# Loading the first chunk of x transposed by DMA instead of transposing it on TensorE

## Chip, core and metric

The kernel runs on one core of one Trainium2 chip. The metric is the device time of one execution, in microseconds. The time of a kernel is the median of several executions.

## What is computed

A dense layer, SiLU, and a second dense layer, all in bf16:

```
x: [1, 2048, 640]    w1: [640, 1728]    w2: [1728, 640]

h   = einsum("bsd,df->bsf", x, w1)
h   = silu(h)                         # h * sigmoid(h)
out = einsum("bsf,fd->bsd", h, w2)    # [1, 2048, 640]
```

TensorE contracts over the 128 partitions of its two operands. For the first layer the contracted dimension is D = 640, five blocks of 128. So w1 can be loaded as it lies in memory, but x, whose rows are tokens, is needed transposed: D on the partitions, tokens along the free dimension. How the transposed x gets into SBUF for the first 512 tokens is what is changed.

## The kernel before

The names used below: P = 128, D = 640 (DT = 5 blocks), F = 1728 padded to FT = 14 blocks, S = 2048 tokens in NSC = 4 chunks of SCH = 512. `xT_sb` holds the transposed x, `w1_sb` and `w2_sb` the weights, `hT_sb` the activated hidden layer (hidden units on partitions), `ps1` four PSUM buffers of the first layer, `ps2` the PSUM of the second.

The first layer is a list of units. A unit computes one block of 128 hidden units for a stretch of tokens, with five accumulating matmuls. The first two blocks of chunk 0 are split in two halves of 256 tokens, so that work can begin on the first half:

```python
w1_groups = [(0, 2), (2, 4), (4, 8), (8, FT)]   # blocks of w1 loaded together
N_W1_ACT = 1                                    # groups loaded on the ScalarE queue
HN = SCH // 2
N_SPLIT_FT = 2
for ft in range(N_SPLIT_FT):
    units.append((0, ft, 0, HN))
TP_INSERT_AFTER = 0
for ft in range(N_SPLIT_FT):
    units.append((0, ft, HN, HN))
for ft in range(N_SPLIT_FT, FT):
    units.append((0, ft, 0, SCH))
# ... then all blocks of chunks 1, 2 and 3, 512 tokens each
```

TensorE first runs warm-up matmuls on zeros, which compute nothing that is used. Then it transposes the first chunk of x by multiplying with an identity matrix, two token blocks ahead of the first unit and two after it, and goes through the units:

```python
for i in range(N_WARM_MM):                      # 11, L246
    pe.matmul(ps1[:, NB1 - 1, :], lhsT=z_sb[:, 0:P], rhs=z_sb[:, :], start=True, stop=True)
...
def transpose_block(j):                         # L260
    if j % 2 == 0:
        pe.wait_ge(sem_x0[j // 2], 16)          # x half loaded
    for dt in range(DT):
        ins = pe.matmul(tp_views[wv][:, sl, :], lhsT=x0_sb[:, j, dt * P:(dt + 1) * P],
                        rhs=ident[:, :], start=True, stop=True)
    ins.then_inc(sem_tp, 1)
...
for i, (sc, ft, c0, n) in enumerate(units):
    # chunk 0: wait until VectorE and ScalarE have copied the transposed blocks
    # other chunks: wait for the five DMA transposes of the chunk
    # wait for the group of w1, and for a free PSUM buffer (sem_dve1)
    for dt in range(DT):                        # L295
        ins = pe.matmul(ps1[:, buf, 0:n], lhsT=w1_sb[:, dt, ft * P:(ft + 1) * P],
                        rhs=xT_sb[:, dt, col0:col0 + n], start=(dt == 0), stop=(dt == DT - 1))
    ins.then_inc(sem_pe1, 1)
    if i == TP_INSERT_AFTER:
        for j in range(hj, JB):
            transpose_block(j)
```

VectorE copies three of the five transposed blocks of each token block from PSUM to `xT_sb` (L414), ScalarE the other two (L363). For each unit ScalarE then computes the sigmoid (L372) and VectorE multiplies it with the matmul's result into `hT_sb` (L422), which also frees the PSUM buffer.

The loads are issued on two queues. SyncE's queue runs in order:

```python
sp.dma_start(out=x0_sb[:, 0:hj, :], in_=x0_v[:, 0:hj, :]).then_inc(sem_x0[0], 16)  # L182
sp.wait_ge(sem_x0[0], 16)
for gi in range(N_W1_ACT, len(w1_groups)):      # L189: groups 1, 2, 3
    load_w1_group(gi)
sp.wait_ge(sem_w1[W1_BIG], 16)                  # group 2 landed
for sc in range(1, NSC):
    x_chunk_transposes(sc)                      # L200: five DMA transposes of 512x128 each
    # after chunk 2: the three loads of w2
```

ScalarE's queue loads the second half of x's first chunk (L348) and group 0 of w1 (L353).

After all units the second layer runs (L335), 16 token tiles over 14 blocks, with its results copied out of PSUM by VectorE (L435, L447) and ScalarE (L384, L396) and stored.

Of the kernel before, what the change touches and what calls it, by code (L numbers as in the profile page):

```python
# [6 lines left out]
ALU = mybir.AluOpType  # L7


def bass_standalone__dense_activation_silu__prompt_kernel(  # L10
# [6 lines left out]
    bf16 = mybir.dt.bfloat16  # L17
    fp32 = mybir.dt.float32

    xf = x.flatten_outer_dims()  # L20
    of = out.flatten_outer_dims()
    S, D = xf.shape
    F = w1.shape[1]
    P = 128
    assert D % P == 0 and S % 512 == 0 and 512 < D <= 1024
    DT = D // P
    FT = (F + P - 1) // P
    FP = FT * P
    F_LAST = F - (FT - 1) * P
    ST = S // P  # L30
    SCH = 512
    NSC = S // SCH
    JB = SCH // P
    NB1 = 4
    NOB = 4
    DA = 512
    DB = D - DA
    assert ST >= 4 and ST % 2 == 0 and (ST - 2) % NOB + 1 == (ST - 1) % NOB
    assert JB % 2 == 0

    w1_groups = [(0, 2), (2, 4), (4, 8), (8, FT)]
    N_W1_ACT = 1
    W1_BIG = 2

    def w1_group_of(ft):
        for gi, (a, b) in enumerate(w1_groups):
# [2 lines left out]
        raise AssertionError  # L49

    HN = SCH // 2
    N_SPLIT_FT = 2
    units = []
    for ft in range(N_SPLIT_FT):
        units.append((0, ft, 0, HN))
    TP_INSERT_AFTER = 0
    for ft in range(N_SPLIT_FT):
        units.append((0, ft, HN, HN))
    for ft in range(N_SPLIT_FT, FT):
# [9 lines left out]
    n_w2_full = FT - 1 if F_LAST != P else FT  # L69
    w2_half = n_w2_full // 2  # L70
    n_w2_dmas = 3 if n_w2_full != FT else 2
    N_INIT = 4 if FP != F else 3
    N_WARM_MM = 11
    TPV = 3
    assert TPV <= 4 and DT - TPV <= 4

    TP_BANKS = {0: (1, 0), 1: (1, 8), 2: (0, 8), 3: (1, 0)}

    def tp_slot(j, dt):
        which, base = TP_BANKS[j % 4]  # L80
        slot = base + dt if dt < TPV else base + 4 + (dt - TPV)
        return which, slot

    with ExitStack() as es:
        def sb(name, shape, dtype):
            return es.enter_context(nc.sbuf_tensor(name, shape, dtype))
# [4 lines left out]
        def sem(name):  # L91
            return es.enter_context(nc.semaphore(name))

        xT_sb = sb("xT_sb", [P, DT, S], bf16)
# [2 lines left out]
        hT_sb = sb("hT_sb", [P, FT, S], bf16)  # L97
        sig_sb = sb("sig_sb", [P, NB1, SCH], bf16)
        o_sb = sb("o_sb", [P, NOB, D], bf16)
        x0_sb = sb("x0_sb", [P, JB, D], bf16)  # L100
        ident = sb("ident", [P, P], bf16)
        warm_sb = sb("warm_sb", [P, 32], fp32)
        z_sb = sb("z_sb", [P, SCH], bf16)
        ps1 = ps("ps1", [P, NB1, SCH], fp32)
        ps2 = ps("ps2", [P, 2, 1024], fp32)
        tp_views = [
            ps1[:, :, :].rearrange("p a (k s) -> p (a k) s", s=P),
            ps2[:, :, :].rearrange("p a (k s) -> p (a k) s", s=P),
        ]

        sem_init = sem("sem_init")
        sem_w2pad = sem("sem_w2pad")
        sem_z = sem("sem_z")
        sem_x0 = [sem(f"sem_x0_{i}") for i in range(JB // 2)]
        sem_x = [None] + [sem(f"sem_x{i}") for i in range(1, NSC)]
        sem_w1 = [sem(f"sem_w1_{i}") for i in range(len(w1_groups))]
        sem_w2 = sem("sem_w2")
        sem_o = [sem(f"sem_o{i}") for i in range(NOB)]
        sem_tp = sem("sem_tp")
        sem_tpc_v = sem("sem_tpc_v")  # L120
        sem_tpc_a = sem("sem_tpc_a")
        sem_pe1 = sem("sem_pe1")
        sem_act1 = sem("sem_act1")
        sem_dve1 = sem("sem_dve1")
# [4 lines left out]
        block = es.enter_context(nc.Block())  # L129

        w1_v = w1.rearrange("(dt p) f -> p dt f", p=P)
        x0_v = xf[0:SCH, :].rearrange("(j p) d -> p j d", p=P)
        w2_full_v = w2[0:n_w2_full * P, :].rearrange("(ft p) d -> p ft d", p=P)

        segs = []
# [21 lines left out]
        @block.gpsimd  # L157
        def _(pool):
            pool.memset(z_sb[:, SCH // 2:SCH], 0.0).then_inc(sem_z, 1)  # L159
            pool.memset(ident[:, :], 0.0).then_inc(sem_init, 1)  # L160
            pool.wait_ge(sem_init, 1)
            pool.affine_select(  # L162
                out=ident[:, :],
                in_=ident[:, :],
                compare_op=ALU.not_equal,
                fill=1.0,
                base=0,
                pattern=[[-1, P]],
                channel_multiplier=1,
            ).then_inc(sem_init, 1)  # L170
            if FP != F:
                pool.memset(w1_sb[:, :, F:FP], 0.0).then_inc(sem_init, 1)  # L172
            pool.memset(warm_sb[:, :], 0.0).then_inc(sem_init, 1)
            if FP != F:
                pool.memset(w2_sb[:, FT - 1, :], 0.0).then_inc(sem_w2pad, 1)  # L175
            else:
                pool.memset(warm_sb[:, 0:1], 0.0).then_inc(sem_w2pad, 1)

        @block.sync
        def _(sp):  # L180
            hj = JB // 2
            sp.dma_start(  # L182
                out=x0_sb[:, 0:hj, :], in_=x0_v[:, 0:hj, :]
            ).then_inc(sem_x0[0], 16)

            def load_w1_group(gi):
                a, b = w1_groups[gi]
# [2 lines left out]
                    out=w1_sb[:, :, f0:f1], in_=w1_v[:, :, f0:f1]  # L190
                ).then_inc(sem_w1[gi], 16)

            sp.wait_ge(sem_x0[0], 16)
            for gi in range(N_W1_ACT, len(w1_groups)):
                load_w1_group(gi)

# [5 lines left out]
                        in_=xf[s0:s0 + SCH, dt * P:(dt + 1) * P],  # L202
                    ).then_inc(sem_x[sc], 16)

            sp.wait_ge(sem_w1[W1_BIG], 16)
            for sc in range(1, NSC):
                x_chunk_transposes(sc)
                if sc == min(2, NSC - 1):
                    sp.dma_start(
                        out=w2_sb[:, 0:w2_half, :], in_=w2_full_v[:, 0:w2_half, :]  # L210
                    ).then_inc(sem_w2, 16)
                    sp.dma_start(
                        out=w2_sb[:, w2_half:n_w2_full, :],
                        in_=w2_full_v[:, w2_half:n_w2_full, :],
                    ).then_inc(sem_w2, 16)
                    sp.wait_ge(sem_w2pad, 1)
                    if n_w2_full != FT:
                        sp.dma_start(
                            out=w2_sb[0:F_LAST, FT - 1, :],
                            in_=w2[n_w2_full * P:F, :],  # L220
# [3 lines left out]
            for st in range(ST - 2):  # L224
# [4 lines left out]
                    out=of[st * P:(st + 1) * P, :], in_=o_sb[:, ob, :]  # L229
# [6 lines left out]
                in_=o_sb[:, obA:obA + 2, 0:DA],  # L236
# [6 lines left out]
        def _(pe):  # L243
# [8 lines left out]
                )  # L252
            pe.wait_ge(sem_init, N_INIT)

            def transpose_block(j):
                if j % 2 == 0:
                    pe.wait_ge(sem_x0[j // 2], 16)
                for dt in range(DT):
                    wv, sl = tp_slot(j, dt)
                    ins = pe.matmul(  # L260
                        tp_views[wv][:, sl, :],
                        lhsT=x0_sb[:, j, dt * P:(dt + 1) * P],
                        rhs=ident[:, :],
                        start=True,
                        stop=True,
                    )
                ins.then_inc(sem_tp, 1)

            hj = JB // 2
            for j in range(hj):  # L270
                transpose_block(j)

            w1_waited = set()
            x_waited = set()
            tpc_waited = 0
            for i, (sc, ft, c0, n) in enumerate(units):
                buf = i % NB1
                col0 = sc * SCH + c0
                if sc == 0:
                    jneed = (c0 + n - 1) // P + 1  # L280
                    if tpc_waited < jneed:
                        pe.wait_ge(sem_tpc_v, jneed)
                        pe.wait_ge(sem_tpc_a, jneed)
                        tpc_waited = jneed
                elif sc not in x_waited:
                    pe.wait_ge(sem_x[sc], 16 * DT)
                    x_waited.add(sc)
                gi = w1_group_of(ft)
                if gi not in w1_waited:
                    pe.wait_ge(sem_w1[gi], 16)  # L290
                    w1_waited.add(gi)
                if i >= NB1:
                    pe.wait_ge(sem_dve1, i - NB1 + 1)
                for dt in range(DT):
                    ins = pe.matmul(  # L295
                        ps1[:, buf, 0:n],
                        lhsT=w1_sb[:, dt, ft * P:(ft + 1) * P],
                        rhs=xT_sb[:, dt, col0:col0 + n],
                        start=(dt == 0),
                        stop=(dt == DT - 1),  # L300
                    )
                ins.then_inc(sem_pe1, 1)
                if i == TP_INSERT_AFTER:
                    for j in range(hj, JB):
                        transpose_block(j)

            pe.wait_ge(sem_w2pad, 1)
            pe.wait_ge(sem_w2, 16 * n_w2_dmas)
# [35 lines left out]

        @block.scalar
        def _(act):
            hj = JB // 2
            act.dma_start(  # L348
                out=x0_sb[:, hj:JB, :], in_=x0_v[:, hj:JB, :]
            ).then_inc(sem_x0[1], 16)  # L350
            for gi in range(N_W1_ACT):
                a, b = w1_groups[gi]
                act.dma_start(  # L353
# [3 lines left out]
            act.activation(  # L357
                out=warm_sb[:, :], in_=warm_sb[:, :], func=ACT.Sigmoid
            )
            for j in range(JB):  # L360
                wv, s0_ = tp_slot(j, TPV)
                act.wait_ge(sem_tp, j + 1)
                act.copy(  # L363
                    out=xT_sb[:, TPV:DT, j * P:(j + 1) * P],
                    in_=tp_views[wv][:, s0_:s0_ + (DT - TPV), :],
                ).then_inc(sem_tpc_a, 1)
            for i, (sc, ft, c0, n) in enumerate(units):
                buf = i % NB1
                act.wait_ge(sem_pe1, i + 1)
# [37 lines left out]
        @block.vector  # L407
        def _(dve):
            dve.memset(z_sb[:, 0:SCH // 2], 0.0).then_inc(sem_z, 1)  # L409
            dve.wait_ge(sem_init, N_INIT)  # L410
            for j in range(JB):
                wv, s0_ = tp_slot(j, 0)
                dve.wait_ge(sem_tp, j + 1)  # L413
                dve.tensor_copy(  # L414
                    out=xT_sb[:, 0:TPV, j * P:(j + 1) * P],
                    in_=tp_views[wv][:, s0_:s0_ + TPV, :],
                ).then_inc(sem_tpc_v, 1)
            for i, (sc, ft, c0, n) in enumerate(units):
                buf = i % NB1
                col0 = sc * SCH + c0  # L420
# [58 lines left out]
```

## Time and profile before

| | before |
|---|---|
| device time, median of 4 | 134.41 us (133.53 to 134.57) |
| span of the profiled execution | 132.8 us |
| PE busy | 127.2 us (96%) |
| first layer's matmuls, L295 | 60.7 us |
| second layer's matmuls, L335 | 60.6 us |
| VectorE busy | 52.0 us (39%) |
| ScalarE busy | 40.5 us (31%) |

PE is TensorE's matmul, PEld its loading of the stationary operand, DVE is VectorE, ACT ScalarE, POOL GpSimd, SP SyncE. A name with q, such as SPq, is the engine's queue of instructions, here the issuing of DMA transfers. Times in the profile count from the start of the span. The profile has a chain of work: from the last instruction of the run it goes back, step by step, to whatever each one waited for. What lies on it sets the time; what lies beside it doesn't, however long it is. Where the profile says "issue" the engine waited for nothing it shows. The times "to landing" count from the issue of a transfer to its completion.

### The profile page before, as it was taken

How to read it: one execution, taken by the hardware profiler on the slowest of the kernel's cores; microseconds unless marked ns; L12 is line 12 of the kernel's file. 1: busy time of each engine (PE TensorE's matmuls, PEld its weight loads, DVE VectorE, ACT ScalarE, POOL GpSimd, SP SyncE). 2: the span in 40 equal slices, each digit the busy share in tenths (PEclk: the TensorE clock that was granted, in tenths of full speed). 3: DMA queues.
4: the chain of work that ended last, by engine and by line, in shares of the span. 5: the costliest groups of instructions: out<-in, count | busy, mean ns of one | idle time of the engine just before them, and what ended most of it. 6: DMA issues, size and time to landing. Idle time of an engine off the chain costs nothing.

```text
span 132.8 us, 1876 instructions
## 1 busy us (share of the span) xinstructions
PE 127.2 (96%) x755; PEld 65.8 (50%) x769; DVE 52.0 (39%) x78; ACT 40.5 (31%) x79; POOL 1.9 (1%) x10
## 2 busy tenths in 40 slices
PE   6969999999999999999999999999999999999992
PEld 2445444444444444444445555555555555555461
DVE  0065666666666666666662222222012222220121
ACT  4054555555555555555550000000000000000001
POOL 5000000000000000000000000000000000000000
PEclk9999999999999999999999999999999999999999
DMA  3898454699400000000000111011111110111103
GB/s 112 250 363 217 110 67 105 168 376 278 82 2 0 5 0 2 0 0 0 0 0 5 49 49 49 15 40 49 49 49 49 54 49 7 42 49 54 49 0 99
DMA packets 15672, 9.78 MB, mean 74 GB/s; under 512 B 8816, under 2 KB 15664, under 8 KB 15664
## 3 DMA queue, kind: packets, MB, share of 16 engines
q1 hardware_dynamic: 14464, 8.95, 23.9%
q10 hardware_dynamic: 1200, 0.72, 1.8%
q8 instruction: 6, 0.10, 0.3%
q14 instruction: 2, 0.02, 0.0%
HBM read 5.08 MB, written 2.62 MB: 58 GB/s over the span
## 4 chain that ended last, share of the span: by engine, by line
PE 95%; DVE 2%; issue 1%; ACT 0%; POOL 0%; DVEq 0%; POOLq 0%
PE ps L335 46%; PE ps L295 45%; PE ps L246 4%; DVE xT_sb L414 2%; PE ps L260 1%; ACT o_sb L396 0%; POOL z_sb L159 0%; DVEq L413 0%; POOLq L464 0%
## 5 line engine op out<-in xcount | busy, mean ns | idle before, releaser
L295 PE MATMUL ps<-xT_sb,w_sb 128*128 128x512 bf16 (+1 forms) x284 | 60.7, 372 | 1.5 <-DVE xT_sb L414 1.2
L335 PE MATMUL ps<-w_sb,hT_sb 128*128 128x512 bf16 (+1 forms) x440 | 60.6, 298 | 0.4
L335 PEld LDWEIGHTS ps<-w_sb,hT_sb 128*128 128x128 bf16 x448 | 34.5, 98 | 26.7
L422 DVE TENSOR_TENSOR hT_sb<-ps,sig_sb 128x512 bf16<-128x512 f32 (+1 forms) x58 | 39.0, 674 | 22.0 <-ACT sig_sb L372 21.9
L295 PEld LDWEIGHTS ps<-xT_sb,w_sb 128*128 128x128 bf16 x290 | 28.2, 98 | 33.5 <-DVE xT_sb L414 1.7
L372 ACT ACTIVATE sig_sb<-ps 128x512 bf16<-128x512 f32 (+1 forms) x58 | 33.7, 583 | 27.0 <-PE ps L295 27.0
L435 DVE CAST o_sb<-ps 128x512 bf16<-128x512 f32 x14 | 9.7, 692 | 42.9 <-PE ps L335 42.9
L384 ACT CAST o_sb<-ps 128x128 bf16<-128x128 f32 x14 | 3.7, 266 | 49.2 <-PE ps L335 49.2
L246 PE MATMUL ps<-z_sb 128*128 128x512 bf16 x11 | 4.9, 632 | 1.1 <-POOL z_sb L159 1.1
L414 DVE CAST xT_sb<-ps 128x384 bf16<-128x384 f32 x4 | 2.0, 553 | 6.7 <-PE ps L260 6.7
L447 DVE CAST o_sb<-ps 128x1024 bf16<-128x1024 f32 x1 | 1.2, 1225 | 5.3 <-PE ps L335 5.3
L246 PEld LDWEIGHTS ps<-z_sb 128*128 128x128 bf16 x11 | 1.5, 143 | 3.6 <-issue 2.5
L363 ACT CAST xT_sb<-ps 128x256 bf16<-128x256 f32 x4 | 1.3, 373 | 4.8 <-PE ps L260 4.8
L396 ACT CAST o_sb<-ps 128x256 bf16<-128x256 f32 x1 | 0.4, 373 | 7.3 <-PE ps L335 7.3
L260 PEld LDWEIGHTS ps<-ident,x_sb 128*128 128x128 bf16 x20 | 1.6, 116 | 0.6 <-issue 0.6
L357 ACT ACT_TABLE_LOAD x1 | 1.3, 1283 | 1.8 <-issue 1.8
L260 PE MATMUL ps<-ident,x_sb 128*128 128x128 bf16 x20 | 1.7, 245 | 0.0
L175 POOL MEMSET w_sb<- 128x640 bf16 x1 | 0.6, 632 | 0.0
L409 DVE MEMSET z_sb<- 128x128 uint32 x1 | 0.2, 165 | 0.8 <-PEq L464 0.8
L172 POOL MEMSET w_sb<- 128x320 bf16 x1 | 0.4, 365 | 0.0
L159 POOL MEMSET z_sb<- 128x256 bf16 x1 | 0.3, 312 | 0.3 <-POOLq L464 0.3
L162 POOL TENSOR_SCALAR_AFFINE_SELECT ident<-ident 128x128 bf16<-128x128 bf16 x1 | 0.3, 295 | 0.2 <-POOL ident L160 0.2
(7 smaller groups left out, 1.0 us busy)
## 6 DMA issues: line engine op xcount, KB each, us to landing
out_dram<-o_sb SPq DMA_DIRECT2D x14, 160.0 KB, 1.8
w_sb<-in_w_dram SPq DMA_DIRECT2D x1, 1120.0 KB, 8.3
w_sb<-in_w_dram SPq DMA_DIRECT2D x1, 960.0 KB, 5.5
w_sb<-in_w_dram SPq DMA_DIRECT2D x1, 880.0 KB, 6.7
w_sb<-in_w_dram SPq DMA_DIRECT2D x1, 640.0 KB, 4.6
x_sb<-in_x_dram SPq DMA_DIRECT2D x1, 320.0 KB, 3.7
x_sb<-in_x_dram ACTq DMA_DIRECT2D x1, 320.0 KB, 4.1
w_sb<-in_w_dram ACTq DMA_DIRECT2D x1, 320.0 KB, 4.5
```

The costliest lines, as they stand in the source:

```text
L246: pe.matmul(ps1[:, NB1 - 1, :], lhsT=z_sb[:, 0:P], rhs=z_sb[:, :], start=True, stop=True,)
L260: ins = pe.matmul(tp_views[wv][:, sl, :], lhsT=x0_sb[:, j, dt * P:(dt + 1) * P], rhs=ident[:, :], start=True, stop=True,)
L295: ins = pe.matmul(ps1[:, buf, 0:n], lhsT=w1_sb[:, dt, ft * P:(ft + 1) * P], rhs=xT_sb[:, dt, col0:col0 + n], start=(dt == 0), stop=(dt == ...
L335: ins = pe.matmul(ps2[:, b2, c0:c0 + ncol], lhsT=hT_sb[:, ft, st * P:(st + 1) * P], rhs=w2_sb[:, ft, d0:d0 + ncol], start=(ft == 0), stop= ...
L357: act.activation(out=warm_sb[:, :], in_=warm_sb[:, :], func=ACT.Sigmoid)
L363: act.copy(out=xT_sb[:, TPV:DT, j * P:(j + 1) * P], in_=tp_views[wv][:, s0_:s0_ + (DT - TPV), :],).then_inc(sem_tpc_a, 1)
L372: act.activation(out=sig_sb[:, buf, 0:n], in_=ps1[:, buf, 0:n], func=ACT.Sigmoid,).then_inc(sem_act1, 1)
L384: act.copy(out=o_sb[:, ob, DA:D], in_=ps2[:, b2, c0:c0 + ncol]).then_inc(sem_ev_a, 1)
L414: dve.tensor_copy(out=xT_sb[:, 0:TPV, j * P:(j + 1) * P], in_=tp_views[wv][:, s0_:s0_ + TPV, :],).then_inc(sem_tpc_v, 1)
L422: dve.tensor_tensor(out=hT_sb[:, ft, col0:col0 + n], in0=ps1[:, buf, 0:n], in1=sig_sb[:, buf, 0:n], op=ALU.mult,).then_inc(sem_dve1, 1)
L435: dve.tensor_copy(out=o_sb[:, ob, 0:DA], in_=ps2[:, b2, c0:c0 + ncol]).then_inc(sem_ev_v, 1)
L447: dve.tensor_copy(out=o_sb[:, obA:obA + 2, 0:DA], in_=ps2[:, bA_, 0:2 * DA].rearrange("p (t c) -> p t c", t=2),).then_inc(sem_ev_v, 1)
```

## The change

The first 512 tokens of x are loaded already transposed, in two DMA transposes of 256 tokens by 640, as the other chunks are loaded transposed in five transfers of 512 by 128. The purpose is to take the transposing off TensorE, and the copies out of PSUM off VectorE and ScalarE, at the start of the kernel. The identity matrix, its making on GpSimd, the staging tensor `x0_sb` and their semaphores go away. Four things are adjusted with it: four blocks instead of two are split into halves of 256 tokens, four more warm-up matmuls run, group 1 of w1 moves from SyncE's queue to ScalarE's, and SyncE no longer waits for transfers to land before it issues the next ones.

```diff
-    N_W1_ACT = 1
-    W1_BIG = 2
+    N_W1_ACT = 2
...
-    N_SPLIT_FT = 2
+    N_SPLIT_FT = 4
...
-    N_INIT = 4 if FP != F else 3
-    N_WARM_MM = 11
+    N_INIT = 2 if FP != F else 1
+    N_WARM_MM = 15
...
         @block.sync
-            hj = JB // 2
-            sp.dma_start(
-                out=x0_sb[:, 0:hj, :], in_=x0_v[:, 0:hj, :]
-            ).then_inc(sem_x0[0], 16)
+            for h in range(2):
+                r0 = h * HN
+                sp.dma_start_transpose(
+                    out=xT_sb[:, :, r0:r0 + HN],
+                    in_=xf[r0:r0 + HN, :].rearrange("s (dt p) -> s dt p", p=P),
+                ).then_inc(sem_xc0[h], 16)
...
-            sp.wait_ge(sem_x0[0], 16)
             for gi in range(N_W1_ACT, len(w1_groups)):
                 load_w1_group(gi)
...
-            sp.wait_ge(sem_w1[W1_BIG], 16)
             for sc in range(1, NSC):
                 x_chunk_transposes(sc)
...
         @block.tensor
-            def transpose_block(j):
-                ... (the identity matmuls)
-            hj = JB // 2
-            for j in range(hj):
-                transpose_block(j)
...
                 if sc == 0:
-                    jneed = (c0 + n - 1) // P + 1
-                    if tpc_waited < jneed:
-                        pe.wait_ge(sem_tpc_v, jneed)
-                        pe.wait_ge(sem_tpc_a, jneed)
-                        tpc_waited = jneed
+                    for h in range(c0 // HN, (c0 + n - 1) // HN + 1):
+                        if ("c0", h) not in x_waited:
+                            pe.wait_ge(sem_xc0[h], 16)
+                            x_waited.add(("c0", h))
...
-                if i == TP_INSERT_AFTER:
-                    for j in range(hj, JB):
-                        transpose_block(j)
...
         @block.scalar
-            act.dma_start(
-                out=x0_sb[:, hj:JB, :], in_=x0_v[:, hj:JB, :]
-            ).then_inc(sem_x0[1], 16)
...
-            for j in range(JB):
-                ... act.copy of two transposed blocks to xT_sb
...
         @block.vector
-            dve.wait_ge(sem_init, N_INIT)
-            for j in range(JB):
-                ... dve.tensor_copy of three transposed blocks to xT_sb
```

In the changed kernel the warm-up matmuls are L211, the first layer's L240, and the transposed loads of chunk 0 L148.

More of the change, by code (lines that the diff above doesn't have):

```diff
@@ L32, in bass_standalone__dense_activation_silu__prompt_kernel @@
     NSC = S // SCH
-    JB = SCH // P
     NB1 = 4
@@ L38, in bass_standalone__dense_activation_silu__prompt_kernel @@
     assert ST >= 4 and ST % 2 == 0 and (ST - 2) % NOB + 1 == (ST - 1) % NOB
-    assert JB % 2 == 0
     w1_groups = [(0, 2), (2, 4), (4, 8), (8, FT)]
-    N_W1_ACT = 1
-    W1_BIG = 2
+    N_W1_ACT = 2
     def w1_group_of(ft):
@@ L55, in bass_standalone__dense_activation_silu__prompt_kernel @@
         units.append((0, ft, 0, HN))
-    TP_INSERT_AFTER = 0
     for ft in range(N_SPLIT_FT):
@@ L71, in bass_standalone__dense_activation_silu__prompt_kernel @@
     n_w2_dmas = 3 if n_w2_full != FT else 2
-    N_INIT = 4 if FP != F else 3
-    N_WARM_MM = 11
[L74 to L82, printed above, removed]
+    N_INIT = 2 if FP != F else 1
+    N_WARM_MM = 15
     with ExitStack() as es:
@@ L99, in bass_standalone__dense_activation_silu__prompt_kernel @@
         o_sb = sb("o_sb", [P, NOB, D], bf16)
-        x0_sb = sb("x0_sb", [P, JB, D], bf16)
-        ident = sb("ident", [P, P], bf16)
         warm_sb = sb("warm_sb", [P, 32], fp32)
@@ L105, in bass_standalone__dense_activation_silu__prompt_kernel @@
         ps2 = ps("ps2", [P, 2, 1024], fp32)
[L106 to L109, printed above, removed]
         sem_init = sem("sem_init")
@@ L113, in bass_standalone__dense_activation_silu__prompt_kernel @@
         sem_z = sem("sem_z")
-        sem_x0 = [sem(f"sem_x0_{i}") for i in range(JB // 2)]
+        sem_xc0 = [sem(f"sem_xc0_{i}") for i in range(2)]
         sem_x = [None] + [sem(f"sem_x{i}") for i in range(1, NSC)]
@@ L118, in bass_standalone__dense_activation_silu__prompt_kernel @@
         sem_o = [sem(f"sem_o{i}") for i in range(NOB)]
-        sem_tp = sem("sem_tp")
-        sem_tpc_v = sem("sem_tpc_v")
-        sem_tpc_a = sem("sem_tpc_a")
         sem_pe1 = sem("sem_pe1")
@@ L131, in bass_standalone__dense_activation_silu__prompt_kernel @@
         w1_v = w1.rearrange("(dt p) f -> p dt f", p=P)
-        x0_v = xf[0:SCH, :].rearrange("(j p) d -> p j d", p=P)
         w2_full_v = w2[0:n_w2_full * P, :].rearrange("(ft p) d -> p ft d", p=P)
@@ L159, in _ @@
             pool.memset(z_sb[:, SCH // 2:SCH], 0.0).then_inc(sem_z, 1)
[L160 to L170, printed above, removed]
             if FP != F:
@@ L253, in _ @@
             pe.wait_ge(sem_init, N_INIT)
-            def transpose_block(j):
[L256 to L267, printed above, removed]
-            hj = JB // 2
-            for j in range(hj):
-                transpose_block(j)
             w1_waited = set()
             x_waited = set()
-            tpc_waited = 0
             for i, (sc, ft, c0, n) in enumerate(units):
@@ L346, in _ @@
         def _(act):
-            hj = JB // 2
-            act.dma_start(
-                out=x0_sb[:, hj:JB, :], in_=x0_v[:, hj:JB, :]
-            ).then_inc(sem_x0[1], 16)
             for gi in range(N_W1_ACT):
@@ L359, in _ @@
             )
-            for j in range(JB):
[L361 to L366, printed above, removed]
             for i, (sc, ft, c0, n) in enumerate(units):
@@ L409, in _ @@
             dve.memset(z_sb[:, 0:SCH // 2], 0.0).then_inc(sem_z, 1)
-            dve.wait_ge(sem_init, N_INIT)
-            for j in range(JB):
[L412 to L417, printed above, removed]
             for i, (sc, ft, c0, n) in enumerate(units):
```

## The prediction

> **What bounds the kernel now.** I read the chain that ended last first, because it says what the end of the run hangs on.
>
> ```profile
> PE 95%; DVE 2%; issue 1%; ACT 0%; POOL 0%; DVEq 0%; POOLq 0%
> PE ps L335 46%; PE ps L295 45%; PE ps L246 4%; DVE xT_sb L414 2%; PE ps L260 1%; ACT o_sb L396 0%; POOL z_sb L159 0%; DVEq L413 0%; POOLq L464 0%
> ```
>
> The reader is to see that 91% of the span is the two layers' matmuls (L295 and L335), which the change leaves alone. Only the small terms can move: warm-up matmuls (L246), identity transposes (L260) and copies out of PSUM (L414), about 7% together. All of these lie in the first 10 us, so I took the same chain in order of time there (start, length, what).
>
> ```profile
> 1.10 4.87 PE ps L246 x11
> 5.97 0.55 PE ps L260 x5
> ...
> 6.62 1.03 DVE xT_sb L414 x2
> 7.65 0.04 issue
> 7.70 0.72 PE ps L295 x5
> 8.42 0.29 PE ps L260 x5
> ...
> 8.73 1.03 DVE xT_sb L414 x2
> 9.77 0.05 issue
> 9.81 1.26 PE ps L295 x10
> ```
>
> The warm-up ends, TensorE transposes, VectorE copies for a microsecond, TensorE does one unit (five matmuls), transposes again, VectorE copies for another microsecond. Only from 9.81 us does layer 1 run without a gap. Ten 256-column matmuls are done by then. A 512-column matmul takes 0.216 us in the steady part: the chain's pieces of L295 repeat every 10.79 us, for 50 matmuls each (49 have a record). Half of it, 0.108 us, times ten is 1.08 us. So the start is worth as much as an unbroken layer 1 from 9.81 - 1.08 = **8.73 us**. I call this the effective start; a microsecond off it is a microsecond off the time, as nothing later waits: layer 1's only idle time ahead of TensorE is 1.2 us, all on these copies.
>
> Next the SyncE queue in the timeline (start, time the queue was held) and the transfers' landing times in the page, for the new first transfers.
>
> ```profile
> 0.73 0.46 SPq L182 DMA_DIRECT2D x_sb<-in_x_dram  x1
> 4.46 1.52 SPq L189 DMA_DIRECT2D w_sb<-in_w_dram  x3
> 9.52 13.86 SPq L200 DMA_TRANSPOSE xT_sb<-in_x_dram  x10
> ```
>
> ```profile
> w_sb<-in_w_dram SPq DMA_DIRECT2D x1, 640.0 KB, 4.6
> xT_sb<-in_x_dram SPq DMA_TRANSPOSE x15, 3.1
> ```
>
> A DMA transpose of 512x128 holds the queue for 1.26 us in the median, where a plain transfer holds it about 0.5 us. It lands about 2.7 us after its start where little else moves (those issued from 12 to 15 us and from 19 to 23 us), and 3.1 in the median of all.
>
> The last view is a table of windows (columns: window and its length, PE, PEld, DVE, ACT and POOL busy, clock, DMA share, GB/s), for how fast the DMA engines can transpose.
>
> ```profile
> 22.00:23.00 1.00, 1.00 (x5) 0.41 (x5) 0.61 (x2) 0.52 (x2) 0.00 (x0) 1.00 0.57 130
> 27.00:28.00 1.00, 1.00 (x7) 0.42 (x5) 0.61 (x2) 0.60 (x1) 0.00 (x0) 1.00 1.07 376
> 33.00:34.00 1.00, 1.00 (x6) 0.42 (x5) 0.67 (x1) 0.52 (x2) 0.00 (x0) 1.00 1.10 215
> ```
>
> Paced by the queue, transposes move 130 GB/s with the engines 57% busy. With a backlog (33 us) they reach 215 GB/s; plain loads (27 us) reach 376.
>
> [...] warm-up weight loads are 0.43 us apart (the loads at 4.06, 4.49 and 4.91 us), twice 0.216. The first ten identity transposes show the switch: nine of their weight loads fill 0.84 us, so eight intervals of 0.0925 us, between the cold 0.107 (a quarter of 0.428) and the 0.061 of the second ten (0.65 us for ten). Solving 0.107 n + 0.061 (8 - n) = 0.74 gives n = 5.5, so full clock from about 5.77 + 5.5 x 0.107 = 6.36 us.
>
> [...] transposes beside the w2 loads took 6.6 and 7.8 us.
>
> [...]
>
> **The change part by part.**
>
> *Removed from the path.* Twenty identity matmuls and eight copies go, with both waits of TensorE on VectorE.
>
> *Warm-up, 11 to 15 matmuls.* At 0.4275 us each the eleven end at 1.10 + 4.70 = 5.80 us. If the clock switches at 6.36, 1.3 of the four added ones run cold and 2.7 take 0.216 us: the array comes free at 6.36 + 0.59 = **6.95 us**. All cold it would be 7.51 us; with an early switch at about 4.5, 8 cold and 7 warm end at 6.0.
>
> *First half of x.* It is 256x640, 2.5 times the elements of a 512x128 transfer. Its issue is either proportional, 2.5 x 1.26 = 3.15 us, or a fixed 0.5 (the plain transfers) plus 2.5 x 0.76 = 2.4 us. Landing came 2.7 - 1.26 = 1.45 us after the issue ended. So 0.73 + (2.4 to 3.15) + 1.45 = 4.6 to 5.3 us undisturbed. Groups 0 and 1 of w1 (0.65 MB at 376 GB/s, 1.75 us of all engines) run beside it; if half of that delays it, about 5.5 to 6.2 us. That is ahead of 6.95, so the wait ends with the warm-up.
>
> *Second half.* Its issue ends at 0.73 + (4.8 to 6.3), it lands at 7.0 to 8.5 us, up to 9 with contention. TensorE has four units on the first half, 20 x 0.108 = 2.16 us, and asks for it at 6.95 + 2.16 = 9.11 us. This is what N_SPLIT_FT = 4 buys: it covers the second transfer. The margin is thin.
>
> *w1 group 2* is issued after both transposes, at 5.5 to 7.0 us. In the kernel before it landed 1.9 us after group 1, which took 3.2 alone for 0.33 MB (0.87 us at 376): 2.3 fixed plus 1.75 is 4.05 us, so 9.6 to 11.1 us. It is needed after eight half units, at 6.95 + 40 x 0.108 = 11.27 us. Again thin. Group 3 has 2.35 us more of data, at most 13.5 us, and is needed at 15.6.
>
> *Later chunks.* Chunk 1's five transposes follow at about 8 us and land by about 16; they are needed one quarter of layer 1 (15.1 us) after the start, at 22. ScalarE (0.386 us per half unit) and VectorE (0.422) stay under TensorE's 0.54 us. Ten whole matmuls become twenty halves, for 0.04 us.
>
> *Sum.* The effective start goes from 8.73 to 6.95, a gain of 1.78 us. I take off 0.1 for the thin margins and get 134.41 - 1.7 = **132.7 us**, 1.3% less.
>
> **The rivals.**
>
> 1. *The transposed load becomes the start's bound.* The wait for VectorE is replaced by one for the DMA. If the 3D transpose costs 4 us of issue, or the first transfers after launch are slower, the halves land at about 6.9 and 10.9; the effective start is then 10.9 - 2.16 = 8.7 and the gain is nothing: 134.4 us. For it: no transpose of this shape is in the trace, and DMA was at full share from 3 to 5 us before. Against it: needed are 9.1 us, and the same bytes at 215 GB/s are 3.05 us plus 1.75 for w1, 4.8 us of transfer from 1.9 us on.
> 2. *w1 group 2 comes late.* Sharing the queue behind two long transposes, it may land at 12 us: a stall of 0.7 us, 133.4 us. For it: it waits for the queue and for bandwidth. Against it: before, it landed at 9.6 having been issued at 5.0.
> 3. *The transposed load is far slower than its share* (5 us or more each, or slowed again by the neighbouring loads as beside w2, 7.8 us): halves at 8 and 13 us, effective start about 11, 136.7 us. Only this reaches a loss near 2%, and nothing but the w2 contention speaks for it.
> 4. *The warm-up costs less.* With the clock switched early, TensorE is free at 6.0, about when the load arrives: a gain of 2.7, or 131.8 us with the same 0.1 off. The same early switch would speed the kernel before too, whose times spread from 133.53 to 134.57.
>
> **Range and chances.** The path has a floor: no load makes TensorE free before about 6.0 to 7.5 us, so the gain is bounded by about 2.7 us, and 2% (2.69 us, below 131.7) is at its very edge. The other side is open, to about no gain where the load decides. So 131.7 to 134.2, faster by over 2% with chance 0.09, within 2% 0.86, slower 0.05.
>
> **What would show it.** In the chain after, the warm-up is 15 matmuls and L240 (the layer-1 matmul there) follows it by 7.0 us, without VectorE between. The transposes hold the queue 2.4 to 3.15 us each. If the first L240 starts well after the last warm-up, or there is a gap after 20 or 40 half matmuls, rival 1 or 2 holds. Layer 2's first matmul, 69.35 us before, should stand near 67.6. A different length of either layer from there would make the whole reckoning wrong.

## The result, and the profile after

| | before | after |
|---|---|---|
| device time, median | 134.26 us (16 runs, 133.28 to 134.60) | 132.94 us (11 runs, 132.79 to 133.18) |
| ratio after to before | | 0.991 (0.9888 to 0.9932) |
| span of the profiled execution | 132.8 us | 131.4 us |
| first matmul of layer 2 | 69.35 us | 67.93 us |

The change gained 1.3 us, 0.9%. The prediction was 132.7 us. The times after lie within 0.4 us of each other, those before within 1.3 us; this turned out to be the clue to what holds the start now.

The chain of the kernel after, shares by engine and by line:

```profile
PE 97%; issue 1%; ACT 0%; POOL 0%; POOLq 0%
PE ps L277 46%; PE ps L240 46%; PE ps L211 5%; ACT o_sb L327 0%; POOL z_sb L135 0%; POOLq L387 0%
```

VectorE is off the chain, and the warm-up's share went from 4 to 5%. The same chain in order of time (start, length, what):

```profile
1.10 6.34 PE ps L211 x15
7.45 4.37 PE ps L240 x40
11.81 0.05 issue
11.86 10.74 PE ps L240 x49
...
67.93 5.43 PE ps L277 x40
```

The chain counts an overlap of two matmuls to the first of them, and their ends are modelled. Layer 1's first matmul began a little earlier, as TensorE's timeline shows (start, length, engine, what):

```profile
7.28 4.96 PE L240 MATMUL ps<-xT_sb,w_sb 128*128 128x256 bf16 x41
```

Layer 1 follows the warm-up and has no gap after 20 or 40 half matmuls. Both layers have their old length: layer 1 takes 60.65 us from 7.28 to the start of layer 2, and took 60.62 from the effective start of 8.73; layer 2's matmuls are 60.6 us as before. So the whole gain lies ahead of layer 1, as expected. The transfers of the kernel after, from the queue's timeline and from the view of the transposed loads' line (queue held, minimum/median/maximum in ns; then landing):

```profile
0.73 4.11 SPq L148 DMA_TRANSPOSE xT_sb<-in_x_dram  x2
4.89 1.44 SPq L156 DMA_DIRECT2D w_sb<-in_w_dram  x2
```

```profile
L148 SPq DMA_TRANSPOSE xT_sb<-in_x_dram x2: 1357/2026/2695, 0.7 to 2.1; - x2
...
DMA to landing us min/median/max: 5.7/6.0/6.3
```

The first half was issued at 0.73 and landed 6.3 us later, at **7.04 us**; the second, issued at 2.15, landed at 7.84. The first is much later than the 5.5 to 6.2 us of the prediction, and close to the 7.28 us at which layer 1's first matmul began. From this view alone one can't tell whether the load or the warm-up let TensorE go. The trace's records of single packets show where the load was. A half of x is 1280 pieces of 256 bytes, a group of w1 640 pieces of 512 bytes:

```
us            x, SyncE's queue (packets)    w1, ScalarE's queue (packets)
1.5 to 3.5              0                        467   group 0
3.5 to 4.5            681   first half           173   group 0
4.5 to 5.5            597   first half           315   group 1
5.5 to 6.0              5                        304   group 1
6.0 to 7.5           1277   second half           21   group 1
completion of the first half: 6.88 to 7.04; of group 1: 6.71 to 6.82
```

No packet of x moved before 3.5 us, when three quarters of group 0 of w1, issued at the same time on the other queue, had passed. The first half's data were through at 5.5 us, but its completion came 1.3 to 1.5 us later, just after that of group 1.

### The profile page after: what moved, and what is told of

It is laid out like the page before. It is cut to its first block, busy times and chain, and to the rows that moved or that the text cites. A ratio compares the mean times of both kernels' runs of the same rounds, so it can differ in the third digit from the quotient of the medians.

```text
span 131.4 us, 1854 instructions
## 1 busy us (share of the span) xinstructions
PE 126.9 (97%) x749; PEld 65.9 (50%) x763; DVE 50.5 (38%) x76; ACT 39.8 (30%) x77; POOL 1.5 (1%) x8
## 4 chain that ended last, share of the span: by engine, by line
PE 97%; issue 1%; ACT 0%; POOL 0%; POOLq 0%
PE ps L277 46%; PE ps L240 46%; PE ps L211 5%; ACT o_sb L327 0%; POOL z_sb L135 0%; POOLq L387 0%
## 5 line engine op out<-in xcount | busy, mean ns | idle before, releaser
L277 PE MATMUL ps<-w_sb,hT_sb 128*128 128x128 bf16 (+1 forms) x440 | 60.6, 298 | 0.4
L240 PE MATMUL ps<-xT_sb,w_sb 128*128 128x512 bf16 (+1 forms) x294 | 60.3, 365 | 0.3
L240 PEld LDWEIGHTS ps<-xT_sb,w_sb 128*128 128x128 bf16 x300 | 29.4, 98 | 31.3 <-issue 0.3
L211 PE MATMUL ps<-z_sb 128*128 128x512 bf16 x15 | 6.3, 615 | 1.1 <-POOL z_sb L135 1.1
L211 PEld LDWEIGHTS ps<-z_sb 128*128 128x128 bf16 x15 | 2.1, 146 | 4.7 <-issue 3.6
```

Of the source, the lines that this page charges most:

```text
L277: ins = pe.matmul(ps2[:, b2, c0:c0 + ncol], lhsT=hT_sb[:, ft, st * P:(st + 1) * P], rhs=w2_sb[:, ft, d0:d0 + ncol], start=(ft == 0), stop= ...
```

## The experiments

Two theories stood against each other. **A**, the prediction's: the warm-up sets the start, the load is in time. **B**: the transposed load, at 7.0 us, sets it wherever the warm-up ends earlier. A third, **C**, gave the gain to the earlier issue of the loads. Ratios are to the kernel before on the same chip, with their 95% intervals.

**Fewer warm-up matmuls.**

```diff
-    N_WARM_MM = 15
+    N_WARM_MM = 11
```

> The changed kernel with 11 warm-up matmuls instead of 15. Theory A (the warm-up sets the start, the load is in time): TensorE starts layer 1 at about 5.9 us, cold, and the time falls to about 132.3. Theory B (the first transposed half, which landed at 7.04 us in the trace of the changed kernel, sets the start as much as the warm-up): TensorE stands still from 5.8 to about 7.1 us, nothing is gained, 132.9 us[...].

Measured: 132.98 us, 0.9913 (0.9882 to 0.9945), as with 15. The chain:

```profile
1.10 4.05 PE ps L211 x11
5.15 1.86 issue
7.01 4.53 PE ps L240 x40
```

The warm-up ended at 5.15 us, the first half of x landed at 6.92, and layer 1 began at 7.01. TensorE stood still for 1.86 us, which the chain calls "issue" because it found nothing to put it down to; the landing just before it says what it was. B holds: where the warm-up ends early, the load sets the start, here 0.09 us after it landed. In the trace of the changed kernel itself the same 0.09 us after the landing would be 7.13 us, but layer 1 began at 7.28: the clock, by the trace's record of it, switched only at 7.07, and the warm-up still ended last, by about 0.15 us.

One of the eight runs took 134.38 us, and two versions below have one such run each (134.34 us among 15 runs, 134.86 us among 22). Those runs have no trace, and the cause is not shown.

**Plain loads in place of the transposed ones.** The 512 tokens are left untransposed.

```diff
-                sp.dma_start_transpose(
+                sp.dma_start(
                     out=xT_sb[:, :, r0:r0 + HN],
-                    in_=xf[r0:r0 + HN, :].rearrange("s (dt p) -> s dt p", p=P),
+                    in_=xf[r0:r0 + HN, :].rearrange("(p a) d -> p (a d)", p=P).rearrange(
+                        "p (dt s) -> p dt s", s=HN),
```

> The changed kernel with the two transposed loads of chunk 0 replaced by plain loads of the same bytes into the same place; the transposition of these 512 tokens is left out, so the output differs from the reference. Theory A (the warm-up alone sets the start): same time as the changed kernel, 132.9 us. Theory B (the transposed load holds the start wherever the warm-up ends earlier): the load lands at about 5 us, the start is set by the warm-up, whose end varies with the moment of the clock's switch, and the times spread again as those of the kernel before do, over about a microsecond below 133.1; median about 132.5.

Measured: 132.65 us (131.57 to 133.13), 0.987 (0.9833 to 0.9906). The chain of its profiled execution, which took 131.57 us:

```profile
1.10 4.71 PE ps L212 x15
5.81 4.42 PE ps L241 x40
```

The first half landed at 5.59 us, and layer 1's first matmul began at 5.68, just as the last one of the warm-up made way (the chain has 5.81). The spread of 1.6 us is back. So the narrow band of the changed kernel is the mark of the load: it arrives at about 7.0 us whenever the clock switches (7.04 with the switch at 7.07, and 7.00 with one at 4.57 in a trace below), and hides the early switches that this run can use. The plain load, too, moved no packet before 3.5 us, so that part of the delay is not the transposing.

**Two split blocks.**

```diff
-    N_SPLIT_FT = 4
+    N_SPLIT_FT = 2
```

> The changed kernel with two blocks split into halves instead of four, so that the second half of x is asked for one microsecond earlier, at about 8.4 us. The prediction's step (four split blocks cover the second transfer, whose margin is thin) with the landing it estimated, 8.5 to 9: a wait of 0.1 to 0.6 us, 133.1 to 133.5 us. Rival, with the landing of the trace (7.84 us): no wait at all, 132.9 us.

Measured: 132.96 us, 0.9899 (0.9874 to 0.9923). No wait: splitting four blocks gains nothing here. With layer 1 starting at 7.15 us, the second half is asked for at 8.2 and is there at 7.9.

**Only the queue changes, in the kernel before.**

```diff
-    N_W1_ACT = 1
+    N_W1_ACT = 2
...
-            sp.wait_ge(sem_x0[0], 16)
...
-            sp.wait_ge(sem_w1[W1_BIG], 16)
```

> The kernel before, with only the queue changes: group 1 of w1 on ScalarE's queue, and no waits of SyncE for transfers to land; x is still transposed on TensorE. Theory A and B (the gain is the round trip over VectorE that goes away): no gain, 134.2 us, or a little worse if the loads of x get in each other's way. Rival C (the earlier issue of the loads gives the gain): about 133.0 us.

Measured: 136.99 us, 1.0211 (1.0174 to 1.0248), worse than any theory said. The chain:

```profile
1.26 7.66 DMA w_sb<-in_w_dram
8.93 0.14 issue
9.06 0.71 PE ps L293 x5
```

Group 0 of w1, issued at 1.26 us, landed only at 8.93: the packets of groups 2 and 3, issued on the other queue from 1.24 us, moved ahead of its own and among them. That makes the first unit 1.36 us later (9.06 us, 7.70 before). The rest of the loss goes with the clock: after TensorE's pause of 2.3 us the clock's record in this trace is back at half from 9.73 to 13.14 us (mean granted clock 0.987, where the other profiled runs have 0.998 or more), and the second ten identity transposes took 1.15 us instead of 0.72. Layer 2 begins at 71.90 us, 2.55 us later than before, so about 1.2 us more were lost in that stretch. C is out: issuing the loads earlier gains nothing, and in the kernel before TensorE waited for VectorE's copies (1.2 us), never for a load. What the waits do is to keep the large loads behind the small urgent ones. The other half of the edit, with both waits kept:

```diff
-    N_W1_ACT = 1
+    N_W1_ACT = 2
```

> The kernel before with group 1 of w1 on ScalarE's queue and both waits of SyncE kept, the half of the queue change that was mixed in the run with no waits (137.0 us). If leaving out the waits did that harm: 134.2 us here, with group 0 of w1 landing by 6 us. If moving group 1 did it: about 137 us.

Measured: 134.28 us, 0.9999 (0.9980 to 1.0017). So the missing waits did the harm. The changed kernel does without them: groups 2 and 3 stand behind both halves of x on the same queue. That the two transposed loads hold the queue until 4.84 us is not needed for it: with plain loads, group 2 was issued at 2.11 us, and its first packet still moved only after 6.5 us.

**The load of x first.** The edit in short:

```diff
-    N_W1_ACT = 2                      # and N_WARM_MM = 15, N_SPLIT_FT = 4
+    N_W1_ACT = 0                      # N_WARM_MM = 11, N_SPLIT_FT = 2
 # SyncE's queue:
-  x half 0, x half 1, w1 groups 2, 3          (groups 0, 1 on ScalarE's queue)
+  x half 0, w1 group 0, x half 1, w1 groups 1, 2, 3
```

> The changed kernel with the load of the first half of x put ahead of all others: SyncE's queue takes, in this order, the first half of x, group 0 of w1, the second half of x, then groups 1, 2 and 3; ScalarE loads nothing; 11 warm-up matmuls, two split blocks. In the changed kernel no packet of the transposed load moved before group 0 of w1, on the other queue, had passed (3.5 us). If that order is what makes the first half land at 7.0 us: it lands at about 5 us, layer 1 starts at 5.2 to 5.9 us, and the time is 131.5 to 132.3 us, with the spread of the clock's switch back in it. If a transposed load simply takes 6 us from the launch: no gain, 132.9 us.

Measured: 132.72 us, 0.991 (0.9875 to 0.9945). The mechanism came out and the gain did not. The landing of the first half, and the waits of TensorE (total, times, longest):

```profile
DMA to landing us min/median/max: 3.6/3.6/3.6
```

```profile
PE ps L242 <- DMA w_sb<-in_w_dram: 0.9, 1, 0.9
```

Alone in front, the same transposed load takes 3.6 us instead of 6.3 and is there at 4.3. But now group 0 of w1 is second and lands at 6.5, and layer 1 needs both. The same with group 1 also ahead of the second half, and four split blocks:

> The same with group 1 of w1 ahead of the second half of x, and four split blocks. The first half again lands at about 5 us and group 1 at about 6; the second half comes last, at about 8, and is asked for about 2.2 us after the start, at about 7.7: 131.5 to 132.5 us, or 132.9 if a transposed load takes 6 us from the launch in any case.

Measured: 132.58 us, 0.990 (0.9874 to 0.9926), started by group 0 at 6.67 us. Both missed what was expected (131.5 to 132.3 and 131.5 to 132.5), for the same reason.

**Group 1 of w1 out of the way.**

```diff
-    N_W1_ACT = 2                      # N_WARM_MM = 15, N_SPLIT_FT = 4
+    N_W1_ACT = 1                      # N_WARM_MM = 11, N_SPLIT_FT = 2
```

With this, group 1 is issued by SyncE after both halves of x.

> The changed kernel with group 1 of w1 back on SyncE's queue, behind both halves of x, 11 warm-up matmuls and two split blocks. In the changed kernel the last packet of the first half was read at 5.5 us, but its completion came at 6.9 to 7.0, while group 1 ran on the other queue from 4.5 to 6.1; alone on its queue (x loaded first) the completion came 0.5 us after the last packet. If group 1 beside it holds the first half back: it lands at about 5.9 us, layer 1 starts then, and the time is about 132.2 us. If it lands at 7.0 all the same: 132.9 us or more.

Measured: 132.34 us, 0.987 (0.9842 to 0.9897). The landing of the two halves, and TensorE's timeline (start, length, engine, what, idle before):

```profile
DMA to landing us min/median/max: 4.7/4.8/5.0
```

```profile
1.10 4.15 PE L211 MATMUL ps<-z_sb 128*128 128x512 bf16 x11 [1.10 <-POOL z_sb L135]
5.79 2.34 PE L240 MATMUL ps<-xT_sb,w_sb 128*128 128x256 bf16 x20 [0.54 <-issue]
8.81 3.41 PE L240 MATMUL ps<-xT_sb,w_sb 128*128 128x512 bf16 x15 [0.68 <-DMA w_sb<-in_w_dram]
```

The first half landed at 5.7 us instead of 7.0, and layer 1 began at 5.79. Taking group 1 off the other queue is what did it (fewer warm-up matmuls and fewer split blocks, each alone, had changed nothing): the first half's packets began at 3.3 us, as they do in other versions with group 1 on the other queue (3.3 to 3.5), but its last data moved 0.5 us earlier and its completion 1.3 us earlier. A new wait of 0.68 us, for group 1 itself, took half of the gain. With four split blocks, which ask for group 1 earlier:

> The same with four split blocks, so that the second half of x is asked for 2.2 us after the start and group 1 of w1 already 1.1 us after it. The first half should land as in the run beside it; group 1, which lands last, at about 8.4 us, then makes a wait of about a microsecond: 132.9 us, against 132.2 for two split blocks. If group 1 lands by 7: 132.2 here too.

Measured: 133.35 us, 0.9947 (0.9927 to 0.9967). The wait grew to nearly twice the microsecond expected:

```profile
PE ps L240 <- DMA w_sb<-in_w_dram: 1.9, 1, 1.9
```

So splitting more blocks is not free: it asks for the next weights sooner. This version also isolates the move of group 1: it differs from the one with 11 warm-up matmuls above in nothing else, and its first half of x landed at 5.50 us, where that one's landed at 6.92. Last, the version with two split blocks and with group 1 cut, so that its first block comes sooner:

```diff
-    w1_groups = [(0, 2), (2, 4), (4, 8), (8, FT)]
+    w1_groups = [(0, 2), (2, 3), (3, 5), (5, 9), (9, FT)]
```

> The version with group 1 of w1 behind both halves of x, 11 warm-up matmuls and two split blocks (132.34 us), with its remaining wait, 0.7 us for group 1, which landed at 8.86 us and was asked for at about 8.0, taken away: group 1 is cut into block 2 alone and blocks 3 and 4, so that block 2 lands about 0.5 us earlier. If that wait is what is left: 131.8 to 132.0 us. If many small rows make the cut group no faster, or the blocks after it come late in their turn: 132.3 us or more.

Measured: **132.00 us** (131.70 to 132.17), 0.9832 (0.9795 to 0.9870), the fastest of all. Layer 1 begins at 5.53 us in its trace; three waits for w1 remain on TensorE's weight loads, 1.3 us in all and 0.6 the longest.

**Fewer warm-up matmuls in the kernel before.**

```diff
-    N_WARM_MM = 11
+    N_WARM_MM = 8
```

> The kernel before with 8 warm-up matmuls instead of 11. Its x lands at 4.4 us, but TensorE is warming up until 5.8. If the warm-up holds the start of the kernel before: the identity matmuls begin at 4.5 us and the time falls by up to 1 us, to about 133.3[...]. If group 0 of w1 (landed at 5.75 us) and the copies hold it[...]: 134.2 us or more.

Measured: 133.35 us, 0.9954 (0.9934 to 0.9974). The chain:

```profile
1.10 3.59 PE ps L246 x8
4.69 0.70 PE ps L260 x5
...
6.56 0.72 PE ps L295 x5
...
8.68 1.48 PE ps L295 x11
```

Everything is 1.1 us earlier than with eleven. About half of what the change brought (0.5% of 0.9%) could be had by deleting three warm-up matmuls: the kernel before was warming up until 5.76 us, while its first half of x had landed at 4.44.

**Larger transposes for the other chunks.**

```diff
-                for dt in range(DT):
-                    sp.dma_start_transpose(out=xT_sb[:, dt, s0:s0 + SCH],
-                        in_=xf[s0:s0 + SCH, dt * P:(dt + 1) * P],
-                    ).then_inc(sem_x[sc], 16)
+                sp.dma_start_transpose(out=xT_sb[:, :, s0:s0 + SCH],
+                    in_=xf[s0:s0 + SCH, :].rearrange("s (dt p) -> s dt p", p=P),
+                ).then_inc(sem_x[sc], 16)
```

> The changed kernel with chunks 1 to 3 loaded by one transpose of 512x640 each, instead of five of 512x128. If the time that a transpose holds the queue grows with its elements (the prediction's step): 5 x 1.26 = 6.3 us for each. If it is a fixed cost for each transpose, as the 1.36 us of the first 256x640 one suggests: 1.4 to 3 us each, more where the transfers ahead are not yet done. The time is 132.9 us in both cases, unless the earlier transfers delay groups 2 and 3 of w1.

Measured: 132.99 us, 0.9927 (0.9901 to 0.9953), no change in time, as expected. The queue was held (chunks 1 and 2, minimum/median/maximum):

```profile
L165 SPq DMA_TRANSPOSE xT_sb<-in_x_dram x2: 3138/4688/6238, 6.4 to 12.6; - x2
```

Neither rule holds. Chunk 2 took 3.1 us, half of five small ones (6.3); chunk 1, issued behind two large loads, took 6.2, and chunk 3, behind the loads of w2, 8.5. The same transfer held the queue for 3.1 to 8.5 us, the longer times behind large loads.

Nothing that layer 1 needs for its start differs here from the changed kernel, and this trace has an early switch of the clock (4.57 us by its record), which the changed kernel's own lacks. TensorE's timeline (the last number is the idle time before):

```profile
1.10 5.11 PE L210 MATMUL ps<-z_sb 128*128 128x512 bf16 x15 [1.10 <-POOL z_sb L135]
7.09 5.17 PE L239 MATMUL ps<-xT_sb,w_sb 128*128 128x256 bf16 x42 [0.88 <-issue]
```

With all fifteen warm-up matmuls done at 6.20 us, TensorE stood still for 0.88 us, until 0.09 us after the first half of x landed at 7.00. So B holds with the warm-up untouched too.

## Why the prediction was right, and where its reasons were wrong

*What goes away* was right: the two waits on VectorE are gone from the chain, and the gain is the difference of two starts of layer 1 and nothing else: 8.73 less 7.28 is 1.45 us, and layer 2 began 1.42 us earlier. The predicted starts differ by 1.78. (The prediction puts all of layer 1's idle time down to the copies; by the page they are 1.2 of 1.5 us, which changes nothing in its sums.)

*The warm-up's end*, 6.95 us, was 7.28 in the trace, and those 0.33 us are nearly the whole difference. It was worked out from the one switch of the clock in the trace before (6.36 us). In the trace after, the weight loads at 6.20 and 6.62 us are still 0.42 us apart, and the clock's record there switches at 7.07. A warm-up in matmuls had no fixed length here: fifteen took from 4.71 us to 6.34 in the traces.

*First half of x* is the step that failed: "about 5.5 to 6.2 us. That is ahead of 6.95, so the wait ends with the warm-up." It landed at 7.04, and in two other traces it let TensorE go: at 7.01 with eleven warm-up matmuls, and at 7.09 with fifteen and an early switch of the clock. Three terms were off. The issue held the queue 1.36 us, not 2.4 to 3.15, which should have made the landing earlier. Two terms more than ate that up: the load's data moved only from 3.5 us, behind most of group 0 of w1, and its completion was held up beside group 1. The prediction had given the contention at most 0.9 us; loading x first shows 2.7 us of difference (6.3 against 3.6), and moving group 1 alone 1.4 us (6.92 against 5.50). The landings that it names, 6.6 and 7.8 us beside the loads of w2, could not show this, since w2 is on the same queue; that loads on the other queue delay the transposes was the author's estimate. That the sum still came out is chance: the load's 7.0 us happens to equal the warm-up's 6.95. Rival 1, the load as bound, was nearer to the truth about the cause, though it expected the second half to hold the start.

*Second half* and *w1 group 2* were right, with more margin than thought: 7.84 us for a need at about 9.4, and 9.8 for 11.6. N_SPLIT_FT = 4 buys nothing in this kernel.

*Rival 4*, an early switch giving 131.8 us, didn't occur in eleven runs, because the load forbids it. It came as soon as the load was out of the way (131.57 with plain loads, the fifteen done at 5.81 us). The switch at about 4.5 us was an estimate that nothing in the trace before showed; 4.57 stands in a trace above.

How the late completion comes about is not shown. From its last data to its completion the transposed load took 1.2 to 1.5 us beside group 1, and 0.4 to 0.7 without it. Beside the same group 1 the plain load's completion came within 0.6 us. So the cause is shown down to group 1 on the other queue, for the transposed load alone, but not the mechanism. In the first 3.5 us most of a load on one queue passed before the other's began, plain or transposed; why is left open.

## What to carry to other kernels

A start that waits for several transfers is set by the last of the set, so reordering only changes which one is last; look for bytes that are not needed yet and move them behind. When a change makes the times more even, ask what new wait hides the old variation. And before crediting a new path with a gain, try the old one with its filler cut to the wait it covers: here three warm-up matmuls less gave half of it.

## What the runs showed of the hardware

By the clock's record, the switch to full clock came at between 3.8 and 7.1 us of the span in the traces, with TensorE busy from 1.1 us in all of them. Fifteen warm-up matmuls took 4.71 us in one trace and 6.34 in another, 1.6 us apart. Where TensorE, and not a transfer, set the start, the times spread by over a microsecond (the kernel before: 133.28 to 134.60 us); that the moment of the switch makes this spread is the author's estimate from those two lengths, as each kernel has one trace. And a pause of 2.3 us was followed by 3.4 us at half clock, in which about 1.2 us more were lost (the version of 136.99 us), while two pauses of 1.9 us were not.

A transposed 256x640 load took 3.6 us to land when nothing was ahead of it, 4.7 to 5.0 behind group 0 of w1, and 6.2 to 6.3 with group 1 beside it as well. A plain load of the same bytes, in pieces of 512 bytes instead of 256, took 4.9 with both groups as neighbours. So the neighbours cost 2.7 us, and the transposing, with its smaller pieces, 1.4 beside them.
